# Attention with the values' products in two column tiles, another order of transfers, and part of VectorE's work elsewhere

## The chip, the core and the metric

One core of a Trainium2 chip runs the whole program. The time is device microseconds of one execution; the figure compared is the median of several executions. A profiled execution has a trace besides, with the start, the length and the releaser of nearly every instruction on the five engines: TensorE (PE; its weight loads are PEld), VectorE (DVE), ScalarE (ACT), GpSimd (POOL) and SyncE (SP, which here only issues transfers).

## The reference

Three layers in a row, all in float32 (the last one's weights come as float64): attention with a window of 128 keys and four sink keys, for 2 batches of 768 positions with 8 heads of 64; a layer of experts, in which each of the 1536 tokens goes to one of 8 experts of 192 places each, in the order of the sorted gate logits; and a dense layer with SiLU.

```
scores = q @ k.T / 8, kept where key < 4 or 0 <= pos_q - pos_k < 128
a = softmax(scores);  x = a @ v                      # [2, 8, 768, 64] -> [1536, 512]
logits = x @ w_gate                                  # [1536, 8]
for idx in argsort(-logits.flatten()):               # greedy, capacity 192 per expert
    tok, e = idx // 8, idx % 8
    if not assigned[tok] and counts[e] < 192: assign tok to e
y[tok] = relu(x[tok] @ w1[e]) @ w2[e]
h = y @ w_in;  out = (h / (1 + exp(-h))) @ w_out
```

## The kernel before

Attention works on 12 tiles of 128 positions with 8 heads each; a half-tile is four heads. One loop (in `attention_band`) runs over steps n, one per head, and each step issues the stages of several heads, each some steps behind the scores:

- `s_mm`, every fourth step: the scores of four heads, in 64x64 tiles of TensorE, 32 matmuls (16 for the first tile of a batch, which has no tile before it), into two PSUM banks out of a ring of four (`s`).
- `s_merge` and `s_max`: VectorE merges the two parts of the window (`copy_predicated`) and takes mask and maximum. `s_exp`, two steps later: ScalarE's exponential.
- `tr`, five steps later: TensorE transposes the exponentials; after four heads, `tr_out` copies them to SBUF on ScalarE (`at`), and GpSimd's two selects cut them into the own tile's part (`atd`) and the tile before's (`at`). `sink_tr`, once per tile: the sinks' exponentials are transposed, and a copy to `ats` is made on VectorE.
- `pv`, 13 steps later, one head a step: one or two matmuls of 128 columns of weights with 73 columns of `va` streamed. The 73 are 64 values, 8 logits (value times gate weights, so that the logits come out of the same product) and a one for the softmax's sum. After the fourth head one product with `vsr` adds the four sinks of all four heads.
- `finish`, after each half-tile: VectorE takes the reciprocal `rv` of the sums (L388), the 32 logits times `rv` (`lw`, L384), the sum of the logits over heads (L391), and the 256 values times `rv` (`x`, L395), which goes to memory with a transfer.

Short work of ScalarE and VectorE that is due soon is put into the deques `act_now` and `dve_now`, other work into `act_bg` and `dve_bg`; `feed` issues one piece at a time at fixed places of a step. `vw`, `vw_tr` and `sinks` (due at the steps of `VWS`) make the logit columns of `va` for two tiles at a time. `warm` issues matmuls on zeros in the first steps.

The float64 weights of the dense layer come as raw pieces in hooks of the same loop, and are unpacked there on VectorE in passes of 128x512 words (`s0` removes the sign, then multiplies and bitwise passes, `s1` on). `FIRST`, `EVEN` and `ODD` are the steps of these hooks: `W.load` asks for a raw piece, `W.unpacked` issues a pass. `load` and `load_v` issue the transfers of a tile on SyncE's queue.

Behind attention the routing repeats an iteration `nit` times with the logits `L_sb`; `foresee` is a hint on the branch that ends it. Then tokens are gathered, and the experts' and the dense layer's matmuls fill the rest.

Of the kernel before, what the change touches and what calls it, by code (L numbers as in the profile page):

```python
# [21 lines left out]
P = 128  # L22
# [5 lines left out]
E = 8  # L28
# [164 lines left out]
WARM = (8,) + (2,) * 5  # L193


def attention_band(tc, qd, kd, va_d, vt_d, vs_d, sel_d, wbd_d, eye_d, n_sink, ident, x_d, L_sb, pp, hooks={}):
    nc = tc.nc
    with ExitStack() as ctx:
# [14 lines left out]
        def load_v(i):  # L213
            b, j = divmod(i, NB)
            if i % 2 == 0:
                vts[i // 2] = wp.tile([P, 4, 2, P], F32, name="vt", bufs=2)
            nc.sync.dma_start(vts[i // 2][:, :, i % 2], vt_d[b, j])
            nc.sync.dma_start(va[:, j], va_d[b, j])
# [131 lines left out]
        def pv(n):  # L350
            i, h = divmod(n, H)
            b, j = divmod(i, NB)
            g, r = divmod(h, 4)
            if r == 0:
                if (i, g) == (NT - 1, 0):
                    X[i, g] = misc(HH * VW).rearrange("p (h v) -> p h v", h=HH)
                else:
                    X[i, g] = pp.tile([P, HH, VW], F32, name="X", bufs=PB["X"])
# [7 lines left out]
            nc.tensor.matmul(X[i, g], ats[i % 2], vsr[b][:, g * HH:(g + 1) * HH], start=False, stop=True,  # L366
                             skip_group_check=True)
            finish(i, g)

        def finish(i, g):  # L370
# [17 lines left out]
            dve_now.append(lambda: nc.vector.reciprocal(rv, xp[:, :, D + E]))  # L388
            dve_now.append(weigh)
            if g == 1:  # L390
                dve_now.append(lambda: nc.vector.tensor_reduce(L_sb[:, i], lw.rearrange("p h e -> p e h"), AX.X,  # L391
                                                               OP.add))
            if i < NT - 2:
                def out():
                    nc.vector.tensor_tensor(x[:, hs], xp[:, :, :D], rv.unsqueeze(2).to_broadcast([P, HH, D]), OP.mult)  # L395
                    act_bg.extend(send)
                dve_bg.append(out)
# [40 lines left out]
        act_now, act_bg, act_late, dve_now, dve_bg = (deque() for _ in range(5))  # L438
        warm(WARM[0])
# [88 lines left out]
class Route:  # L528
# [188 lines left out]
    def run(self, L, idx, nit, more, bg=lambda k: None, speculate=lambda: None):  # L717
        self.place(self.psum("s"))
        for k in range(nit):
            bg(k)  # L720
            if k + 1 == nit:
                self.foresee("settled")
            self.iterate(NA, HOLD[0] if k == 0 else 0)
            self.warm(HOLD[1 + (k + 1 == nit)])
            if k == 0:
                self.scaled()
        bg(nit)
        badi = self.result(idx)
        speculate()
        self.warm(HOLD[3])  # L730
        self.further(badi, L, idx, more, speculate, "settled")
# [155 lines left out]
FIRST, EVEN, ODD = 18, (34, 40, 46, 58, 64, 70, 76, 82, 86), (*range(27, 49, 2), *range(53, 93, 2))  # L887


class Weights:  # L890
# [28 lines left out]
    def unpack(self, k, half):  # L919
# [4 lines left out]
        for part in range(2):  # L924
# [599 lines left out]
def fused(tc, a, out, n_sink, window):  # L1524
    nc = tc.nc
    with ExitStack() as ctx:
# [18 lines left out]
        with rest:  # L1545
# [3 lines left out]
            if banded(n_sink, window):  # L1549
                pp = rest.enter_context(tc.tile_pool(name="p", bufs=1, space=PSUM))  # L1550
                hooks = {NT * H // 2: [load_route]}
                for k in range(W.raws):
                    hooks.setdefault(FIRST + 2 * k, []).append(W.load)
# [147 lines left out]
```

## Time and profile before

| | us |
|---|---|
| median of three runs | 552.18 (551.89 to 552.75) |
| the profiled execution's own time | 551.16 |
| its span in the trace | 549.4 |
| PE busy (share of the span) | 529.3 (96%) |
| VectorE busy | 352.0 (64%) |
| ScalarE busy | 293.2 (53%) |
| GpSimd busy | 228.5 (42%) |

The busy times are means over stages that differ: attention ends at about 98 us, the routing iterations and the gathers of tokens at about 131, the experts at about 285, and the dense layer takes the rest. TensorE's 96% says nothing about which engine the others wait for in attention; this is read from busy times by stretch and from the instructions in order of time. In an order of time, the time of one instruction is its own length, and the start of the next may lie inside it; where one engine's instructions follow each other without a wait, the distance of their starts is what one costs.

### The profile page before, as it was taken

How to read it: one execution, taken by the hardware profiler on the slowest of the kernel's cores; microseconds unless marked ns; L12 is line 12 of the kernel's file. 1: busy time of each engine (PE TensorE's matmuls, PEld its weight loads, DVE VectorE, ACT ScalarE, POOL GpSimd, SP SyncE). 2: the span in 40 equal slices, each digit the busy share in tenths (PEclk: the TensorE clock that was granted, in tenths of full speed). 3: DMA queues.
4: the chain of work that ended last, by engine and by line, in shares of the span. 5: the costliest groups of instructions: out<-in, count | busy, mean ns of one | idle time of the engine just before them, and what ended most of it. 6: DMA issues, size and time to landing. Idle time of an engine off the chain costs nothing.

```text
span 549.4 us, 10689 instructions
## 1 busy us (share of the span) xinstructions
PE 529.3 (96%) x3901; PEld 480.2 (87%) x3901; DVE 352.0 (64%) x983; ACT 293.2 (53%) x576; POOL 228.5 (42%) x219
## 2 busy tenths in 40 slices
PE   8999899878999999999999999999999999999995
PEld 4788688757999999999999998988889899888884
DVE  3798999672443443343338898777979776853523
ACT  4555555655776776786654564443544344443330
POOL 4444354377699999999992000000000000000304
PEclk9999999799999999999999999999999999999999
DMA  7999843155466666666760554553676756265502
GB/s 213 359 391 320 278 162 110 39 197 161 153 210 217 226 227 219 227 222 222 226 184 1 209 201 161 215 161 108 219 263 219 277 173 225 91 241 203 202 17 115
DMA packets 43939, 107.98 MB, mean 197 GB/s; under 512 B 4650, under 2 KB 12458, under 8 KB 43884
## 3 DMA queue, kind: packets, MB, share of 16 engines
q1 hardware_dynamic: 41696, 100.88, 54.1%
q0 software_dynamic: 1920, 6.29, 3.3%
q8 instruction: 31, 0.51, 0.4%
q14 instruction: 24, 0.20, 0.1%
q10 hardware_dynamic: 268, 0.10, 0.1%
HBM read 86.81 MB, written 20.45 MB: 195 GB/s over the span
## 4 chain that ended last, share of the span: by engine, by line
PE 69%; issue 4%; POOL 2%; DMA 1%; ACT 0%; DVE 0%; POOLq 0%; another core or an unknown queue 0%; DVEq 0%; ACTq 0%
PE h L1294 21%; PE acc L1416 21%; PE mm L1200 9%; PE m L1223 8%; PE mm L1203 4%; PE m L1226 4%; POOL out L1387 2%; PE mm L1223 1%; PE mm L1159 1%; DMA row<-x_d,idx 1%; PE mm L1226 1%; PE m L1200 0%; POOLq L1697 0%; PE m L1159 0%; ACT wr L976 0%
## 5 line engine op out<-in xcount | busy, mean ns | idle before, releaser
L979 POOL TENSOR_TENSOR wr<-raw,wr 128x1024 fp32r<-128x1024 f32 x64 | 150.8, 2386 | 9.1 <-ACT wr L976 8.9
L1416 PE MATMUL acc<-wr,gt 128*128 128x512 f32 x576 | 145.4, 395 | 0.0
L1416 PEld LDWEIGHTS acc<-wr,gt 128*128 128x128 f32 x576 | 107.3, 188 | 19.5
L1387 POOL DMA_INDIRECT out<-raw,idx x12 | 11.6, 964 | 241.4 <-DVE raw L1428 241.1
L1294 PE MATMUL h<-x,wr 128*128 128x384 f32 x528 | 101.3, 338 | 0.0
L1294 PEld LDWEIGHTS h<-x,wr 128*128 128x128 f32 x528 | 93.8, 188 | 4.0 <-DVE keep L1328 0.2
L1200 PE MATMUL mm<-xg,wr 128*128 128x384 f32 x248 | 72.4, 360 | 0.5 <-DVE xg L1174 0.3
L976 ACT ACTIVATE wr<-raw 128x1024 fp32r<-128x1024 f32 x64 | 66.8, 1052 | 2.4 <-DMA raw<-in_w 1.3
L1223 PE MATMUL m<-ht,wr 128*128 128x384 f32 x224 | 66.0, 361 | 0.0
L1203 PE MATMUL mm<-xg,wr 128*128 128x192 f32 x248 | 62.2, 251 | 0.0
L1226 PE MATMUL m<-ht,wr 128*128 128x192 f32 x224 | 56.2, 251 | 0.0
L1475 DVE TENSOR_TENSOR gt<-keep,gt 128x384 fp32r<-128x384 f32 x64 | 39.1, 612 | 26.7 <-ACT gt L1281 26.6
L301 ACT ACTIVATE A<-t,nm 128x132 f32<-128x132 f32 x96 | 36.4, 401 | 24.7 <-DVE nm L292 24.4
L1181 DVE TENSOR_TENSOR mm<-mm,t 128x384 f32<-128x384 f32 x33 | 18.7, 566 | 45.2 <-ACT t L1180 45.2
L1200 PEld LDWEIGHTS mm<-xg,wr 128*128 128x128 f32 x248 | 46.5, 188 | 1.2 <-DVE xg L1174 0.7
L1203 PEld LDWEIGHTS mm<-xg,wr 128*128 128x128 f32 x248 | 47.3, 191 | 0.0
L1280 ACT ACTIVATE keep<-keep 128x384 f32<-128x384 f32 x30 | 15.8, 526 | 54.0 <-DVE keep L1328 53.9
L1226 PEld LDWEIGHTS m<-ht,wr 128*128 128x128 f32 x224 | 42.8, 191 | 0.0
L1223 PEld LDWEIGHTS m<-ht,wr 128*128 128x128 f32 x224 | 42.0, 188 | 0.0
L323 POOL TENSOR_SCALAR_AFFINE_SELECT atd<-at 128x512 f32<-128x512 f32 x24 | 17.0, 708 | 50.8 <-ACT at L321 45.7
L1294 PE MATMUL h<-xn,wr 128*128 128x384 f32 x180 | 36.8, 339 | 0.0
L1294 PEld LDWEIGHTS h<-xn,wr 128*128 128x128 f32 x180 | 32.6, 188 | 2.6
(198 smaller groups left out, 931.9 us busy)
## 6 DMA issues: line engine op xcount, KB each, us to landing
raw<-in_w SPq DMA_DIRECT2D x64, 512.0 KB, 4.7
sums_d<-os SPq DMA_DIRECT2D x36, 256.0 KB, 2.0
xn<-mix_d SPq DMA_DIRECT2D x12, 768.0 KB, 5.7
raw<-in_wi SPq DMA_DIRECT2D x16, 512.0 KB, 4.8
raw<-in_wo SPq DMA_DIRECT2D x16, 512.0 KB, 4.7
os<-sums_d SPq DMA_DIRECT2D x24, 256.0 KB, 3.1
mix_d<-xn SPq DMA_DIRECT2D x6, 768.0 KB, 4.7
va<-in_va SPq DMA_DIRECT2D x12, 292.0 KB, 6.1
```

Of the source, the lines that this page charges most:

```text
L301: nc.scalar.activation(A[i][:, h], t, AF.Exp, bias=nm, scale=-1.0)
L976: nc.scalar.activation(w[:, 0, sl], src(), AF.Copy)
L979: (nc.vector if k in self.late else nc.gpsimd).tensor_tensor(w[:, 1, sl], src(), w[:, 0, sl].bitcast(F32), OP.subtract)
L1181: nc.vector.tensor_tensor(h, h, t, OP.add)
L1200: nc.tensor.matmul(mm[:, b, :2 * CAP], w[:, 0, fb, d, o:o + P], x[:, d].rearrange("p a t -> p (a t)"), start=d == 0, stop=False, skip_grou ...
L1203: nc.tensor.matmul(mm[:, b, :CAP], w[:, 1, fb, d, o:o + P], x[:, d, 0], start=False, stop=d == 3, skip_group_check=True)
L1223: nc.tensor.matmul(mm[:, d % 2, :2 * CAP], w[:, 0, d // 2, f, o:o + P], ht[:, f].rearrange("p a t -> p (a t)"), start=c == 0 and f == 0, s ...
L1226: nc.tensor.matmul(mm[:, d % 2, :CAP], w[:, 1, d // 2, f, o:o + P], ht[:, f, 0], start=False, stop=last, skip_group_check=True)
L1294: nc.tensor.matmul(h, w(a, d), x(b, d), start=start and d == 0 and k == 0, stop=d == n - 1 and k == 2, skip_group_check=True)
L1387: i = nc.gpsimd.indirect_dma_start(out=out, out_offset=bass.IndirectOffsetOnAxis(ap=idx[:, t // 3, t % 3:t % 3 + 1], axis=0), in_=o, in_of ...
L1416: nc.tensor.matmul(a, gt[:, u, ts], w[:, v, 2 * p + i], start=(p, i, k) == (0, 0, 0), stop=(p, i, k) == (1, 1, 2), skip_group_check=True)
L1475: later.popleft()()
```

## The change

The values' products of four heads are issued together, at every fourth step, ahead of the next scores (`pv`); each product of 128 output rows becomes two of 64, on two column tiles of TensorE. The sinks' product (`pv_sink`) follows behind the scores. The sinks' copy goes to ScalarE for all tiles. For the tiles up to the eighth, `finish` copies the whole half-tile to SBUF on ScalarE (`xc`), VectorE takes the reciprocal of the copy, GpSimd makes both products, and the sum over heads follows four steps later; the last four tiles keep the old way. The sign removal of the early pieces becomes an absolute value on ScalarE. `load_v` is split, its transfers are put into another order, and the raw pieces of the weights are asked for at other steps, the later ones later. The warm-up matmuls are cut into five pieces each, the steps of `vw` and `vw_tr` are shifted by two and one, and the branch hint is given one iteration sooner.

```diff
-    VWS[2 * H * m + 5], VWS[2 * H * m + 8] = [((m,), 0)], [((m,), 1)]
+    VWS[2 * H * m + 7], VWS[2 * H * m + 9] = [((m,), 0)], [((m,), 1)]
...
-        load_v(0)
+        load_vt(0)
+        load_va(0)
         nc.sync.dma_start(vsf[0][:96], vs_d[:96, 0])
-        load_v(1)
+        load_vt(1)
         load(2)
+        load_va(1)
...
-                nc.tensor.matmul(idle, zero[:, :P], zero, start=True, stop=True)
+                for sl in map(slice, WE, WE[1:]):
+                    nc.tensor.matmul(idle[:, sl], zero[:, :P], zero[:, sl], start=True, stop=True)
...
-            if i < NT - 1:
-                dve_now.appendleft(lambda: nc.vector.tensor_copy(ats[i % 2][:96], tp))
-            else:
-                act_now.appendleft(lambda: nc.scalar.activation(ats[i % 2][:96], tp, AF.Copy))
+            act_now.appendleft(lambda: nc.scalar.activation(ats[i % 2][:96], tp, AF.Copy))
...
-            o = X[i, g][:, r]
-            nc.tensor.matmul(o, d[:, r], va[:, j, h], start=r == 0, stop=False, skip_group_check=True)
-            if j:
-                nc.tensor.matmul(o, f[:, r], va[:, j - 1, h], start=False, stop=False, skip_group_check=True)
-            if r < 3:
-                return
+            for r in range(HH):
+                for t, c in ((d, j), (f, j - 1))[:2 if j else 1]:
+                    for q in (slice(HB), slice(HB, P)):
+                        nc.tensor.matmul(X[i, g][q, r], t[:, r, q], va[:, c, h + r], start=r == 0 and t is d,
+                                         stop=False, skip_group_check=True)
+
+        def pv_sink(n):
...
+            if i >= NT - 4:
+...
+            xc = wp.tile([P, HH, VW], F32, name="xc", bufs=3)
+
+            def taken():
+                nc.scalar.activation(xc, xp, AF.Copy)
+                at_step[now[0] + 1].append(over)
+
+            def over():
+                nc.vector.reciprocal(rv, xc[:, :, D + E])
+                for o, w in ((lw, slice(D, D + E)), (x, slice(D))):
+                    nc.gpsimd.tensor_tensor(o[:, hs], xc[:, :, w],
+                                            rv.unsqueeze(2).to_broadcast([P, HH, w.stop - (w.start or 0)]), OP.mult)
+                if g == 1:
+                    at_step[now[0] + 4].append(logits)
                     act_bg.extend(send)
+            act_now.append(taken)
...
+            dve_now.extend(at_step.pop(n, ()))
+            of = n - LP - HH + 1
+            due = of % HH == 0 and 0 <= of < NH
+            if due:
+                pv(of)
-            if n < NH and n % 4 == 0:
+            if n < NH and n % HH == 0:
                 s_mm(n)
+            if due:
+                pv_sink(of)
...
-                if i == 1:
+                if i == 4:
                     nc.sync.dma_start(vsf[1][:96], vs_d[:96, 1])
-                if i + 2 < NT:
-                    load_v(i + 2)
+                if i % 2 == 0:
+                    load_vt(i + 2)
+                    load_vt(i + 3)
                 if i + 3 < NT:
                     load(i + 3)
+                load_va(i + 2)
...
-            if 0 <= n - LP < NH:
-                pv(n - LP)
...
-            if k + 1 == nit:
+            if k + 2 == nit:
                 self.foresee("settled")
...
-FIRST, EVEN, ODD = 18, ...
+FIRST, EVEN, ODD = (17, 25, 33, 45, 53, 60, 67), ...
...
-                nc.vector.tensor_scalar(box[0][:, sl], word(1), 0x7FFFFFFF, None, OP.bitwise_and)
+                if k in self.early:
+                    nc.scalar.activation(box[0][:, sl].bitcast(F32), word(1).bitcast(F32), AF.Abs)
+                else:
+                    nc.vector.tensor_scalar(box[0][:, sl], word(1), 0x7FFFFFFF, None, OP.bitwise_and)
```

TensorE before, in the middle of attention, from the last score of a half-tile on (`tp` are the transposes of the exponentials, `X` the values' products, L366 the sinks' product):

```order
L264 MATMUL s<-kall,qr 64x132
L315 MATMUL tp<-ident,A 128x128
L414 MATMUL s<-ident,vwt 128x128 x2
L361 MATMUL X<-va,atd 128x73
L363 MATMUL X<-va,at 128x73
L366 MATMUL X<-vsr_157,ats_172 128x292
L315 MATMUL tp<-ident,A 128x128
L361 MATMUL X<-va,atd 128x73
L363 MATMUL X<-va,at 128x73
```

One transpose and one head's products take turns until the next scores. TensorE after, at the same place:

```order
L270 MATMUL s<-kall,qr 64x132
L372 MATMUL X<-vsr_156,ats_172 128x292
L321 MATMUL tp<-ident,A 128x128 x2
L442 MATMUL s<-ident,vwt 128x128 x2
L321 MATMUL tp<-ident,A 128x128 x2
L366 MATMUL X<-va,atd 64x73 x2
L366 MATMUL X<-va,at 64x73 x2
```

The last two rows stand four times, once for each head, and then come the next scores: the transposes now stand together, and the products together behind them, in pairs of 64 output rows.

VectorE before, with the reciprocal and the two products of a finished half-tile (`rv`, `lw`, `x`) between score maxima (L292) and merges (L284):

```order
L388 RECIPROCAL rv_902<-X_833 128x4
L292 ISA t_915,nm_916<-s_859,mask_162 128x132
L292 ISA nm_916 128x1
L384 TENSOR_TENSOR lw_901<-X_833,rv_902 128x32
L284 COPY_PREDICATED s_858<-later_158,s_858 128x128
L284 COPY_PREDICATED s_859<-later_158,s_859 128x128
L395 TENSOR_TENSOR x_900<-X_833,rv_902 128x256
L292 ISA t_929,nm_930<-s_858,mask_162 128x132
L292 ISA nm_930 128x1
L933 TENSOR_SCALAR f64_934<-raw_521 128x512
```

VectorE after, at such a place (L977 and L989 are passes that unpack weights):

```order
L989 SCALAR_TENSOR_TENSOR f64_1468<-raw_1021,f64_1468 128x512
L417 RECIPROCAL rv_1587<-xc_1588 128x4
L298 ISA t_1611,nm_1612<-s_1569,mask_162 128x132
L298 ISA nm_1612 128x1
L290 COPY_PREDICATED s_1568<-later_158,s_1568 128x128
L290 COPY_PREDICATED s_1569<-later_158,s_1569 128x128
L298 ISA t_1623,nm_1624<-s_1568,mask_162 128x132
L298 ISA nm_1624 128x1
L977 TENSOR_SCALAR f64_1468<-f64_1468 128x512
```

The reciprocal stays between the maxima and now reads the copy; both products and the sign removal (L933) are gone from this engine. ScalarE after, in a stretch with all three kinds of work that came to it:

```order
L307 ACTIVATE A_1372<-t_1388,nm_1389 128x132
L307 ACTIVATE A_1372<-t_1438,nm_1439 128x132
L352 ACTIVATE ats0_171<-s_1458 96x128
L971 ACTIVATE f64_1468<-raw_1021 128x512
L307 ACTIVATE A_1372<-t_1454,nm_1455 128x132
L307 ACTIVATE A_1372<-t_1465,nm_1466 128x132
L413 ACTIVATE xc_1506<-X_1475 128x292
L327 ACTIVATE at_1516<-tp_1449 128x512
```

Between the exponentials (L307) and the copy of the transposes (L327), which were there, stand the sinks' copy (L352), the sign removal (L971) and the copy of the finished half-tile (L413).

## Rows read from the trace of the kernel before

**Rows 1.** Busy us (instructions) of each engine by stretch; then clock, DMA share, GB/s.

```profile
14.00:30.00 16.00, 14.88 (x231) 13.09 (x231) 12.24 (x71) 9.35 (x29) 6.91 (x15) 1.00 1.07 366
30.00:75.50 45.50, 42.58 (x629) 37.27 (x628) 43.48 (x218) 25.52 (x70) 19.96 (x41) 1.00 0.90 310
75.50:88.00 12.50, 12.21 (x179) 10.45 (x182) 12.48 (x67) 6.88 (x20) 6.01 (x12) 1.00 0.32 111
20.00:40.00 20.00, 19.59 (x295) 17.31 (x296) 17.07 (x94) 11.63 (x32) 8.71 (x19) 1.00 1.05 388
```

**Rows 2.** TensorE in order of time: start, length, line, operation, shape.

```profile
26.69 0.92 PE L264 MATMUL s<-kall,qr 64*64 64x128 f32 x32
27.54 0.33 PE L315 MATMUL tp<-ident,A 128*128 128x128 f32 x1
27.70 0.34 PE L361 MATMUL X<-va,atd 128*128 128x73 f32 x2
...
28.07 0.38 PE L366 MATMUL X<-vsr,ats 97*128 97x292 f32 x1
28.29 0.27 PE L315 MATMUL tp<-ident,A 128*128 128x128 f32 x1
28.40 0.27 PE L344 MATMUL s<-ident,a 128*96 128x128 f32 x1
28.51 0.34 PE L361 MATMUL X<-va,atd 128*128 128x73 f32 x2
...
28.91 0.27 PE L315 MATMUL tp<-ident,A 128*128 128x128 f32 x1
...
30.02 1.45 PE L264 MATMUL s<-kall,qr 64*64 64x128 f32 x32
```

**Rows 3.** TensorE in order of time, in a first tile of a batch.

```profile
48.72 0.68 PE L264 MATMUL s<-kall,qr 64*64 64x132 f32 x16
49.33 0.33 PE L315 MATMUL tp<-ident,A 128*128 128x128 f32 x1
...
50.39 0.64 PE L403 MATMUL s<-vt,wbd 128*32 128x256 f32 x8
```

**Rows 4.** VectorE in order of time: start, length, line, operation, shape.

```profile
41.27 0.18 DVE L384 TENSOR_TENSOR lw<-X,rv 128x32 f32<-128x32 f32 x1
41.37 0.48 DVE L284 COPY_PREDICATED s<-later,s 128x128 f32<-128x128 int32 x2
41.76 0.41 DVE L395 TENSOR_TENSOR x<-X,rv 128x256 f32<-128x256 f32 x1
42.10 0.28 DVE L292 CUSTOM_DVE_ANT_0 t<-s,mask 128x132 f32<-128x132 f32 x1
...
42.31 0.42 DVE L933 TENSOR_SCALAR f<-raw 128x512 int32<-128x512 int32 x1
42.64 0.28 DVE L292 CUSTOM_DVE_ANT_0 t<-s,mask 128x132 f32<-128x132 f32 x1
...
45.38 0.28 DVE L346 CAST ats<-s 96x128 fp32r<-96x128 f32 x1
45.58 0.28 DVE L292 CUSTOM_DVE_ANT_0 t<-s,mask 128x132 f32<-128x132 f32 x1
```

**Rows 5.** Groups by line, 30 to 88 us: count, busy us, mean ns, idle before.

```profile
L326 POOL TENSOR_SCALAR_AFFINE_SELECT at<-at 128x512 f32<-128x512 f32 x14 | 10.6, 759 | 1.0
L321 ACT ACTIVATE at<-tp 128x512 f32<-128x512 f32 x15 | 8.9, 593 | 8.9 <-PE tp L315 8.9
```

**Rows 6.** TensorE in order of time, with idle time before and its releaser.

```profile
16.60 0.90 PE L264 MATMUL s<-kall,qr 64*64 64x128 f32 x28 [0.52 <-DVE ats L346]
```

**Rows 7.** TensorE behind the routing, in order of time.

```profile
129.85 0.66 PE L1159 MATMUL mm<-ident,row 128*128 128x128 f32 x4 [0.54 <-DMA row<-x_d,idx]
```

**Rows 8.** A select on GpSimd and a pass on VectorE beside it.

```profile
36.02 0.63 POOL L323 TENSOR_SCALAR_AFFINE_SELECT atd<-at 128x512 f32<-128x512 f32 x1 [0.92 <-ACT at L321]
36.16 0.77 DVE L937 TENSOR_SCALAR f<-f 128x512 f32<-128x512 f32 x1
```

More of the change, by code (lines that the diff above doesn't have):

```diff
@@ L1 @@
 import math
-from collections import deque
+from collections import defaultdict, deque
 from functools import partial
@@ L190 @@
 for m in range(1, NT // 2):
-    VWS[2 * H * m + 5], VWS[2 * H * m + 8] = [((m,), 0)], [((m,), 1)]
+    VWS[2 * H * m + 7], VWS[2 * H * m + 9] = [((m,), 0)], [((m,), 1)]
 PB = {"s": 4, "tp": 2, "X": 2}
-WARM = (8,) + (2,) * 5
+WARM, WE = (8,) + (2,) * 5, (0, 104, 208, 312, 412, 512)
 def attention_band(tc, qd, kd, va_d, vt_d, vs_d, sel_d, wbd_d, eye_d, n_sink, ident, x_d, L_sb, pp, hooks={}):
@@ L211, in load, with load_vt, load_va @@
                 nc.sync.dma_start(Q[i][:, p:p + step], qd[b, j][:, p:p + step])
-        def load_v(i):
-            b, j = divmod(i, NB)
+        def load_vt(i):
+            if i >= NT:
+                return
             if i % 2 == 0:
                 vts[i // 2] = wp.tile([P, 4, 2, P], F32, name="vt", bufs=2)
-            nc.sync.dma_start(vts[i // 2][:, :, i % 2], vt_d[b, j])
-            nc.sync.dma_start(va[:, j], va_d[b, j])
+            nc.sync.dma_start(vts[i // 2][:, :, i % 2], vt_d[i // NB, i % NB])
+        def load_va(i):
+            if i < NT:
+                nc.sync.dma_start(va[:, i % NB], va_d[i // NB, i % NB])
         load(0, 1)
@@ L352, in pv @@
             b, j = divmod(i, NB)
[L353 to L358, printed above, removed]
-            f, d = AT[i, g]
-            o = X[i, g][:, r]
-            nc.tensor.matmul(o, d[:, r], va[:, j, h], start=r == 0, stop=False, skip_group_check=True)
-            if j:
-                nc.tensor.matmul(o, f[:, r], va[:, j - 1, h], start=False, stop=False, skip_group_check=True)
-            if r < 3:
-                return
-            nc.tensor.matmul(X[i, g], ats[i % 2], vsr[b][:, g * HH:(g + 1) * HH], start=False, stop=True,
+            g = h // HH
+            if (i, g) == (NT - 1, 0):
+                X[i, g] = misc(HH * VW).rearrange("p (h v) -> p h v", h=HH)
+            else:
+                X[i, g] = pp.tile([P, HH, VW], F32, name="X", bufs=PB["X"])
+            f, d = AT[i, g]
+            for r in range(HH):
[4 more added lines that the diff above has]
+        def pv_sink(n):
+            i, h = divmod(n, H)
+            g = h // HH
+            nc.tensor.matmul(X[i, g], ats[i % 2], vsr[i // NB][:, g * HH:(g + 1) * HH], start=False, stop=True,
                              skip_group_check=True)
@@ L386, in weigh, with logits, out @@
                     act_late.extend([partial(scaled, r) for r in range(HH)] + send)
[L388 to L395, printed above, removed]
+            def logits():
+                nc.vector.tensor_reduce(L_sb[:, i], lw.rearrange("p h e -> p e h"), AX.X, OP.add)
+            if i >= NT - 4:
+                dve_now.append(lambda: nc.vector.reciprocal(rv, xp[:, :, D + E]))
+                dve_now.append(weigh)
+                if g == 1:
+                    dve_now.append(logits)
+                if i < NT - 2:
+                    def out():
+                        nc.vector.tensor_tensor(x[:, hs], xp[:, :, :D], rv.unsqueeze(2).to_broadcast([P, HH, D]),
+                                                OP.mult)
+                        act_bg.extend(send)
+                    dve_bg.append(out)
+                return
+            xc = wp.tile([P, HH, VW], F32, name="xc", bufs=3)
[7 more added lines that the diff above has]
+                                            rv.unsqueeze(2).to_broadcast([P, HH, w.stop - (w.start or 0)]), OP.mult)
+                if g == 1:
+                    at_step[now[0] + 4].append(logits)
                     act_bg.extend(send)
-                dve_bg.append(out)
+            act_now.append(taken)
         def vw(m, os=(0, 1)):
@@ L438, in attention_band @@
         act_now, act_bg, act_late, dve_now, dve_bg = (deque() for _ in range(5))
+        at_step, now = defaultdict(list), [0]
         warm(WARM[0])
@@ L442, in attention_band @@
             i, h = divmod(n, H)
-            if n < NH and n % 4 == 0:
+            now[0] = n
+            dve_now.extend(at_step.pop(n, ()))
[4 more added lines that the diff above has]
+            if n < NH and n % HH == 0:
                 s_mm(n)
+            if due:
+                pv_sink(of)
             if n < len(WARM) - 1:
@@ L886 @@
 PLAIN, MIXED = "uuddduuddd", "ududududududu"
-FIRST, EVEN, ODD = 18, (34, 40, 46, 58, 64, 70, 76, 82, 86), (*range(27, 49, 2), *range(53, 93, 2))
+FIRST, EVEN, ODD = (17, 25, 33, 45, 53, 60, 67), (34, 40, 46, 58, 64, 70, 76, 82, 86), (*range(27, 49, 2), *range(53, 93, 2))
 class Weights:
@@ L1551, in fused @@
                 hooks = {NT * H // 2: [load_route]}
-                for k in range(W.raws):
-                    hooks.setdefault(FIRST + 2 * k, []).append(W.load)
+                for n in FIRST:
+                    hooks.setdefault(n, []).append(W.load)
                 for n in sorted({*EVEN, *ODD}):
```

1 line of the change is left out of this document (added).

## The prediction, made before the changed kernel was run

> **What bounds the kernel now.** I read the clock and busy shares by stretch first, then the two fullest engines' instructions in order of time, then what the other engines' operations cost. Everything behind 98 us (the routing iterations, the gathers, the expert and dense layers) is left as it was by the change, apart from one branch hint, so the question is how much sooner attention hands over. In its middle, 30.0 to 75.5 us, VectorE is busy 43.5 of 45.5 us and TensorE 42.6, at the full clock [rows 1]; those 45.5 us hold twelve half-tiles of four heads, 3.79 us each. From 14 to 30 us VectorE has slack (12.2 of 16.0) and TensorE little (14.9); from 75.5 to 88 us VectorE has none (12.48 of 12.50). So in the middle two engines bind almost equally: freeing one alone gives next to nothing, and the change frees both.
>
> On TensorE one half-tile without waits takes 3.33 us, 26.69 to 30.02 [rows 2]: the scores 0.85, the sink product 0.22 (28.07 to 28.29), a transpose 0.11 (28.29 to 28.40), and the values' products of one head 0.40 (28.51 to 28.91; four records of 73 columns, each with a 128-column load). Two score groups of the twelve are stretched, the first to 1.45 us against 0.92 [rows 2]: there TensorE waits for VectorE to free a score bank. Without these 1.0 us TensorE needs 42.6 - 1.0 = 41.5 us for the twelve.
>
> **The values' products (TensorE).** Before, four heads cost 4 x 0.40 = 1.60 us. After, each product is two of 64 output columns, on two column tiles: twice the records (32 of 73 columns), which gains only if the two tiles run at the same time. The trace has no such pair of 128-row tiles, but near ones. Scores of a first tile: 16 records of 132 columns in 0.61 us (48.72 to 49.33), so each of four tiles streams 4 x 132 = 528 columns [rows 3]; scores of another tile: 32 records in 0.85 us, 784 columns per tile [rows 2]. The difference, 0.24 us for 256 columns, is 0.94 ns a column, and 0.115 us stay fixed. And the eight records of 256 columns on four column tiles (128 rows each) take 0.64 us [rows 3], where one after the other they would need eight times 256 x 0.94 ns, 1.9 us: column tiles over the same rows do stream together. Two tiles with 16 records each: 1168 columns x 0.94 + 0.115 = 1.21 us. I take this; it saves 0.39 us per half-tile. The ends: if a record of half the load costs half of today's 0.10, 16 x 0.05 + 0.115 = 0.92 us; if the tiles load one at a time, 32 x 0.05 + 0.115 = 1.72 to 1.9 us, which is a loss. Half-tiles of a first tile (no second source) gain some 0.05. Sum over the twelve: 10 x 0.39 + 2 x 0.05 = 4.0, so TensorE's need falls to 37.5 us.
>
> The fixed 0.115 us stands for the change between tile shapes, and rows show it again: the transpose behind the scores takes 0.16 until the next product where others take 0.11 [rows 2]. [...] There is now one more change per half-tile, which the 0.115 holds.
>
> **VectorE.** Its operations are issued back to back, so what counts is the time to the next start [rows 4]: the logit product 0.10 (41.27 to 41.37), the normalising product 0.34 (41.76 to 42.10), the sink copy 0.20 (45.38 to 45.58), sign removal 0.33 (42.31 to 42.64). Eight of twelve tiles lose the two products (0.44 a half-tile), all but the last tile lose the sink copy, and the eight pieces of sign removal go. In the middle: 12 x 0.44 + 6 x 0.20 + 6 x 0.33 = 8.5 us, so VectorE needs 43.5 - 8.5 = 35.0. The reciprocal stays, now reading a copy.
>
> **Where that work goes.** ScalarE gets a copy of 128x292 per half-tile, the sink copies and eight 128x512 sign removals. Its 128x512 copy takes 0.59 [rows 5]: 0.3 to 0.6 for the 292, up to 0.6 for the signs, so 12 x 0.45 + 6 x 0.25 + 6 x 0.55 = 10 us on top of 25.5 busy, 36 of the 40 us then left. GpSimd gets two products; its 128x512 select takes 0.76 [rows 5], so 0.4 to 0.8 for the 256 wide and 0.2 to 0.3 for the 32 wide, some 11 us on 20.0. Neither is the fullest, but no engine has much room any more. Cover for the longer way to the logits: they are reduced four steps later, a half-tile of time; the last four tiles keep the old way, so nothing is added at the end.
>
> **What twelve half-tiles take.** Today 2.0 us more than the fuller engine's 43.5. With 37.5 and 35.0, and two more hand-overs in the ring, I allow 2.5: 40.0, a gain of 5.5 us (no loss at all would be 8.0; a loss of 4 would be 4.0). **Before them** (14 to 30 us): two half-tiles with two sources, 0.8, and two waits in one score group, 0.8 together, the larger one 0.52 for the sink copy [rows 6], which now comes from ScalarE; of 1.6 I take 1.3, since other chains are just behind (at least 0.5). **Behind them**, 75.5 to 88 us, VectorE alone binds: two sink copies and one sign removal, 0.7 us. From 88 us on: nothing; there the counts of the first iteration now stand behind a whole group of products and its sink instead of behind three heads, and the group is shorter by as much.
>
> **Edits at no price.** The warm-up matmuls are cut in five but stream the same 512 columns. The transfers: tile data are asked for three tiles ahead, and weights' raw pieces later; from 14 to 75.5 us the queues move 366 and 310 GB/s [rows 1], 20.0 MB; at 388, the mean of the 20 us from 20.0 on [rows 1], that would take 51.5 us where the forecast leaves 54.7, so transfers don't bind, though not by much. The hint one iteration sooner: behind the branch TensorE's transposes wait for the gathered rows, not for code (0.54 us, released by the transfer [rows 7]), and that covers it; without this cover it could give some tenths.
>
> Sum: 5.5 + 1.3 + 0.7 = 7.5 us against the profiled execution's own 551.16 us (span 549.4), so 543.7; the median of the runs lies 1.0 above the profiled one, so **544.7 us**.
>
> **Rivals.** (a) *The hand-overs eat the gain.* VectorE's reciprocal now waits for ScalarE's copy, which waits for the sink product, which stands behind the group's products and the next scores on TensorE; score maxima are queued behind that reciprocal, and exponentials behind the copy. And GpSimd's work slows VectorE's weight unpacking: a 128x512 pass takes 0.77 us when a select runs beside it (36.02 and 36.16 us) [rows 8], another one 0.42 (42.31 us) [rows 4]. With 0.3 us of this per half-tile VectorE needs 38.6, and with a loss of 3.5 the twelve take 42: gain 3.4 + 1.0 + 0.2, 547.6 us. For it: four engines all at 85% or more. Against: the reciprocal stands half a microsecond of other VectorE work behind the scores. [...] (b) *The tiles load one at a time: slower.* Place: the two 64-column loads of each pair, over the same 128 rows. Price: 1.9 us per four heads instead of 1.60. TensorE then needs 41.5 + 10 x 0.3 + 2 x 0.28 = 45.1, with its 2.0 of loss 47.1 for the twelve, 1.6 more than now; before them 0.3 is gained, behind them 0.7 less 0.9 in the last products: 553.7 us. It decides from about 1.75 us per four heads on. Against it: the column-tiled rows of 256 columns [rows 3]; for it, that these hide short loads behind long streams, and 73 columns don't. [...] (c) *Half overlap*: 1.5 us per four heads, TensorE hardly better, only the waits and the end gain: 551 us.
>
> **How the numbers follow.** Forecast 0.66, (a) 0.16, (b) 0.10, (c) 0.08. A run of three rounds tells about 0.2% (1.1 us) from no change. Faster by more: the forecast, (a) and half of (c): 0.86. Within: the rest of (c) and a little of (b), 0.05. Slower: 0.09. The forecast's own bounds: gains of 4.0 + 0.5 + 0.5 (547.2) to 8.0 + 1.6 + 0.7 (541.9), a little lower if records cost 0.05. The range takes in (a) and stops short of (b): 540.5 to 550.5.
>
> **What would show it.** Right: four heads of products in 1.1 to 1.3 us; half-tiles of 3.2 to 3.4 us in the middle; VectorE with idle gaps ended by TensorE or ScalarE; the first routing iteration some 7 us sooner, and everything behind it shifted by the same. Wrong: products of four heads at 1.6 us or more; reciprocals that wait half a microsecond each; or a routing stage that starts sooner but ends no sooner, because weights come late.

## The result: slower by 0.7% where 1.4% faster was forecast

The changed kernel takes 556.07 us (median of nine executions, 553.24 to 557.16) against 551.89 us of before in the same rounds; the ratio is 1.007, with a 95% interval of 1.0049 to 1.0091. The forecast was 544.7 us, within 540.5 to 550.5, with 0.09 for slower. The profiled execution took 556.25 us, its span is 554.5 us.

Busy time by stretch after, as in [rows 1] (columns as there), and two stretches of 6 us behind them:

```profile
14.00:30.00 16.00, 13.52 (x289) 10.55 (x278) 10.39 (x60) 9.80 (x32) 7.95 (x19) 0.99 1.06 368
30.00:75.50 45.50, 41.62 (x830) 33.88 (x831) 37.22 (x182) 32.08 (x96) 31.19 (x65) 0.93 0.92 317
75.50:88.00 12.50, 11.08 (x227) 8.47 (x223) 11.59 (x57) 7.99 (x24) 6.83 (x13) 1.00 0.40 138
...
28.00:34.00 6.00, 4.19 (x68) 3.62 (x69) 2.26 (x12) 3.37 (x10) 2.12 (x4) 0.72 0.59 231
56.00:62.00 6.00, 5.91 (x93) 5.13 (x93) 3.88 (x15) 2.12 (x8) 2.12 (x5) 0.72 1.00 355
```

The work went where the change sent it: VectorE's 43.48 us of the middle are 37.22 now, ScalarE has 32.08 instead of 25.52, GpSimd 31.19 instead of 19.96. But the twelve half-tiles take 43.2 us (32.66 to 75.83) instead of 45.4 (30.02 to 75.46), where 40.0 were forecast, and the granted clock, 1.00 before in all three stretches, is 0.72 on average in two stretches of 6 us.

The values' products on TensorE after (start, length, line, operation, shape), to be held against 0.40 us a head in [rows 2]:

```profile
24.95 0.35 PE L366 MATMUL X<-va,atd 128*64 128x73 f32 x4
25.12 0.30 PE L366 MATMUL X<-va,at 128*64 128x73 f32 x4
...
25.89 0.30 PE L366 MATMUL X<-va,at 128*64 128x73 f32 x4
26.11 0.38 PE L270 MATMUL s<-kall,qr 64*64 64x128 f32 x4
```

32 records stand between 24.95 and 26.11: four heads cost 1.16 us, and 1.21 were forecast. So the column tiles do what was expected of them, and the loss must lie elsewhere. Two milestones show where. The last scores of attention end at 89.29 us (before 88.78), and the last product of the routing at 126.56 (125.55): attention and routing lose 1.0 us where they should gain 7.5. From there to the first transposes of gathered rows it takes 7.92 us (before 4.30): 3.6 us more, in a stretch in which nothing seemed to be changed. TensorE at these places, after:

```profile
88.37 0.92 PE L270 MATMUL s<-kall,qr 64*64 64x128 f32 x32
...
126.37 0.19 PE L882 MATMUL X<-neg,N 128*128 128x8 bf16 x2
...
130.51 4.18 PE L1195 MATMUL mm<-wr 128*128 128x512 f32 x9 [3.05 <-DVEq L780]
134.48 1.06 PE L1199 MATMUL mm<-ident,row 128*128 128x128 f32 x4
```

And before (its first transposes, at 129.85, are in [rows 7]):

```profile
87.87 0.91 PE L264 MATMUL s<-kall,qr 64*64 64x128 f32 x32
...
125.36 0.19 PE L845 MATMUL X<-neg,N 128*128 128x8 bf16 x2
...
126.98 2.33 PE L1155 MATMUL mm<-wr 128*128 128x512 f32 x9 [0.53 <-DVEq L743]
```

L780 (L743 before) is the branch that ends the routing. TensorE waits 3.05 us instead of 0.53, for VectorE's sequencer; its granted clock falls from 1.00 to 0.50 in that wait (0.50 from 129 to 135 us), and the same nine warm-up matmuls, which stand ahead of the transposes, then take 4.18 us instead of 2.33. VectorE's own rows at this line (count, duration in ns, first and last start in us), after, and before:

```profile
L780 DVEq EVENT_SEMAPHORE  x2: 21/21/21, 130.3 to 130.5; - x2
...
L780 DVEq COMPARE_BRANCH  x1: 72/72/72, 127.2 to 127.2; - x1
```

```profile
L743 DVEq EVENT_SEMAPHORE  x2: 21/21/21, 126.8 to 126.9; - x2
...
L743 DVEq COMPARE_BRANCH  x1: 72/72/72, 126.2 to 126.2; - x1
```

VectorE branches at 127.2 and does its next step at 130.3; before, 0.6 us lay between the two.

### The profile page after: what moved, and what is told of

It reads as the page before. It is cut to its first block, busy times and chain, and to the rows that moved or that the text cites. A ratio compares the mean times of both kernels' runs of the same rounds, so it can differ in the third digit from the quotient of the medians.

```text
span 554.5 us, 11517 instructions
## 1 busy us (share of the span) xinstructions
PE 526.0 (95%) x4325; PEld 474.8 (86%) x4325; DVE 342.4 (62%) x932; ACT 301.9 (54%) x611; POOL 242.7 (44%) x251
## 4 chain that ended last, share of the span: by engine, by line
PE 68%; issue 4%; POOL 2%; DMA 1%; DVE 0%; ACT 0%; POOLq 0%; another core or an unknown queue 0%; DVEq 0%; ACTq 0%
PE h L1334 21%; PE acc L1456 20%; PE mm L1240 9%; PE m L1263 8%; PE mm L1243 4%; PE m L1266 4%; POOL out L1427 2%; PE mm L1263 1%; PE mm L1199 1%; PE mm L1266 1%; DMA raw<-in_w 1%; POOL wr L1019 0%; POOL row L1157 0%; PE m L1240 0%; POOLq L1737 0%
## 5 line engine op out<-in xcount | busy, mean ns | idle before, releaser
L307 ACT ACTIVATE A<-t,nm 128x132 f32<-128x132 f32 x96 | 35.3, 401 | 11.3 <-DVE nm L298 10.8
L1321 ACT ACTIVATE gt<-keep 128x384 fp32r<-128x384 f32 x64 | 33.7, 527 | 2.0
```

Of the source, the lines that this page charges most:

```text
L307: nc.scalar.activation(A[i][:, h], t, AF.Exp, bias=nm, scale=-1.0)
L1321: nc.scalar.activation(gt[:, 0], h, AF.Copy)
```

## Experiments on the wait behind the branch

**The hint.** It had been moved, so it was undone alone and done alone:

```diff
-            if k + 2 == nit:
+            if k + 1 == nit:
                 self.foresee("settled")
```

> The changed kernel with the branch hint given where it stood before, in the last iteration. Theory A (the hint given sooner costs the gap of 3 us behind the branch in the trace of after): 552 to 553 us, and the matmuls behind the branch start about 1.5 us after the last product of the routing, as in the kernel before. Rival B (the gap comes from the longer instruction stream of TensorE, 848 rows more in attention): no change, 556 us.

> The kernel before with only the hint one iteration sooner. Theory A: 3 to 4 us slower than before, some 555.3 us, all of it behind the branch. Rival B: no change, 552 us.

Measured: 556.26 us (ratio 1.0082, 1.0053 to 1.0112) and 551.51 us (1.0001, 0.998 to 1.0022). Theory A fell: the wait is there with either place of the hint, and the hint alone changes nothing, as the prediction had priced it.

**The place of the branch in TensorE's program.** The page counts transfers of instructions: 31 on queue q8, 0.51 MB, before and 35, 0.57 MB, after, so some 16 KB each, and four more for the 848 additional records of TensorE in the trace (8650 against 7802, so about 250 records to one of them; a row here is one instruction of an engine's program). Two kernels shift TensorE's rows, by the warm-up pieces alone:

```diff
-WE = (0, 104, 208, 312, 412, 512)
+WE = (0, 172, 344, 512)                # e5; e6: five pieces put into the kernel before
```

> The changed kernel with each warm-up matmul cut in three pieces instead of five: 72 rows fewer ahead on TensorE, so that the branch behind the routing lies as many rows past a multiple of 256 (67) as in the kernel before (66; in the changed kernel 139). Theory C (TensorE's instructions come in transfers of 16 KB, 256 rows, and whether the code behind the branch is there in time hangs on where the branch lies among them): the matmuls behind the branch start 0.5 us after it waits for nothing else, not 3 us, they run at the full clock, and the time falls by 3 to 4 us, to 552.5 us. Rival D (the longer stream as such, or the transfers of that time, make the code late): the gap of 3 us stays, 556 us.

> The kernel before with only the warm-up matmuls cut in five pieces, 144 rows more ahead on TensorE, the same columns. Theory C: the branch now lies 210 rows past a multiple of 256, in another place among the transfers of code, and a gap of 3 us behind the branch is likely: 555 us. Rival D (attention's other edits are needed for the gap): 552 us, gap 0.5 us.

e5: 554.44 us (1.0052, 1.0025 to 1.008), and VectorE's wait is unchanged; theory C was wrong for the changed kernel. TensorE's own branch even takes 1.48 us in e5, against 0.41 after, though it now stands where theory C wanted it. e6: 555.16 us (1.0077, 1.0044 to 1.0111), though the routing ends as before (125.66 us). In e6 it is TensorE's own branch that takes 2.9 us, 0.48 in the kernel before:

```profile
L744 DVEq EVENT_SEMAPHORE  x2: 21/21/21, 126.9 to 127.0; - x2
...
L744 PEldq COMPARE_BRANCH  x1: 2881/2881/2881, 125.8 to 125.8; - x1
```

So each engine can be late behind the branch, by itself (VectorE by 3.1 us after, TensorE's branch with 2.9 us in e6), and on TensorE 144 rows more with the same work were enough.

**VectorE's rows.** The change takes 79 rows off VectorE's program ahead of the branch, which stands at row 529 instead of 608. They were put back as writes of one element, or VectorE got the hint too:

```diff
+        for _ in range(79):
+            nc.vector.memset(spare, 0.0)
```

```diff
-        pe = [mybir.EngineType.PE]
+        pe = [mybir.EngineType.PE, mybir.EngineType.DVE]
```

> The changed kernel with 79 one-element writes on VectorE in its idle first 5 us, so that its branch behind the routing lies at the same row as in the kernel before (608 instead of 529, target 827). Theory J (the wait of 3 us behind the branch is VectorE's: it branches at 127.31 us, its next instruction comes at 130.34, and TensorE waits for it and then runs its warm-up matmuls at half clock; whether VectorE's code is there depends on the row of the branch): VectorE goes on 0.5 us after its branch, TensorE starts with it, and the time falls by 3.5 to 4.5 us, to some 552 us, no better than before. Rival K (VectorE waits for something else behind the branch): gap and time stay, 556 us.

> The changed kernel with the branch hint given to VectorE as well as to TensorE. Theory J (VectorE's code comes late): the hint brings it in time, VectorE goes on within 0.6 us of its branch, 552 us. Rival K: no change, 556 us; so too if the hint has no effect on VectorE's code.

f1 (553.66 us; 1.0017, 0.9993 to 1.0041), VectorE in order of time, and its rows at the branch:

```profile
1.14 8.92 DVE L343 MEMSET spare_v<- 1x1 f32 x79
10.12 0.29 DVE L298 CUSTOM_DVE_ANT_0 t<-s,mask 128x132 f32<-128x132 f32 x1
```

```profile
L783 DVEq EVENT_SEMAPHORE  x2: 21/21/21, 129.9 to 130.0; - x2
...
L783 DVEq COMPARE_BRANCH  x1: 72/72/72, 129.3 to 129.3; - x1
```

The wait is gone (0.6 us), as theory J says; but 79 writes at 113 ns overran the idle time, and the first maximum came at 10.12 instead of 6.10 us, so f1 gives back part of it at the start. f2 changed nothing (555.71 us; 1.0064, 1.004 to 1.0089; VectorE goes on 3.6 us after its branch): a hint given to VectorE has no effect here.

The trace counts the instruction transfers of each queue. Those that begin in VectorE's wait in the changed kernel, from 127.2 to 130.4 us (packets, MB, share of the transfer engines' time; q8 is the queue that grew with TensorE's rows):

```profile
q8 instruction: 1, 0.02, 2.2%
q14 instruction: 2, 0.02, 1.9%
```

So code does come in during the wait, but no transfer of it begins in the wait's last 1.5 us (from 128.9 us on). Whether VectorE waits for any of these transfers isn't shown.

## Experiments on attention

**Single waits.** After, ScalarE and TensorE at 28 us (idle time and its releaser in brackets), and TensorE at two later waits:

```profile
28.81 0.66 ACT L971 ACTIVATE f<-raw 128x512 f32<-128x512 f32 x1 [2.70 <-DMA raw<-in_wi]
```

```profile
29.81 0.77 PE L321 MATMUL tp<-ident,A 128*128 128x128 f32 x2 [2.00 <-ACT A L307]
...
50.89 0.32 PE L351 MATMUL s<-ident,a 128*96 128x128 f32 x1 [0.68 <-POOL a L313]
...
56.09 0.38 PE L452 MATMUL s<-va,sel 4*96 4x64 f32 x2 [1.21 <-ACT va L445]
```

ScalarE's first sign removal waits for the raw piece, the exponentials are queued behind it, and TensorE runs dry for 2.0 us; its mean granted clock from 28 to 34 us is 0.72. From 56 to 62 us it is the same behind waits of 0.68 and 1.21 us. Three kernels (all but e8 with the hint as before) each took one cause away:

```diff
-                if k in self.early:                                       # e3: signs on VectorE
-                    nc.scalar.activation(..., AF.Abs)
+                nc.vector.tensor_scalar(..., OP.bitwise_and)
...
-    VWS[2 * H * m + 7], VWS[2 * H * m + 9] = ...                          # e4
+    VWS[2 * H * m + 5], VWS[2 * H * m + 8] = ...
...
-FIRST = (17, 25, 33, 45, 53, 60, 67)                                      # e8, with load_vt, load_va
+FIRST = (18, 20, 22, 24, 26, 28, 30)                                      # and vsf[1] as before
```

> Hint as before, and the sign removal of the early weights back on VectorE; all else as in the changed kernel. Theory A (ScalarE stands 2.7 us behind the first raw piece, exponentials are queued behind it, TensorE runs dry for 2.0 us and its granted clock then falls to half): ScalarE's wait is gone, no fall of the clock near 30 us, about 4 us faster than the same kernel with the signs on ScalarE, some 548.5 us. Rival B (VectorE then waits for the same piece with maxima queued behind it, and TensorE runs dry all the same): 552 to 553 us and the clock falls near 30 us as before.

> Hint as before, and the products for the logit columns (two tiles at a time) back at their earlier steps, 5 and 8 instead of 7 and 9. Theory A (the sinks' product of the second batch, due at step 58, waits 1.2 us for columns that now come one step ahead of it; TensorE's clock falls after that wait): no such wait near 55 us, no fall of the clock near 57 us, 2 to 3 us faster than the same kernel with the later steps, some 550 us. Rival B (the wait of 0.7 us for GpSimd's part of the sinks at 50 us is enough, or VectorE is what TensorE waits for there): within 0.5 us of it, 552.5 us.

> The changed kernel with the transfers in the order of before: values and their columns tile by tile, the second batch's sinks early, raw pieces asked for from step 18 on every second step. Theory G (the new order makes the first raw piece and a values' transfer land late, TensorE waits for them and its clock falls): ScalarE's wait of 2.7 us for the raw piece is under 1.2 us, no fall of the clock before 50 us, routing ends 3 us sooner, 553 us. Rival H (the engines' new hand-overs make the waits, not the order of transfers): the clock falls as in after, 556 us.

555.30 us (1.0058, 1.003 to 1.0085), 554.77 (1.006, 1.0036 to 1.0085) and 555.25 (1.0072, 1.0027 to 1.0118): none can be told from the changed kernel, nor e3 and e4 from e1. The wait for the first raw piece is gone from e3's profile, but TensorE waits at 12 us for a transfer and the clock falls there instead:

```profile
12.51 0.60 PE L431 MATMUL s<-vt,wbd 128*32 128x128 f32 x8 [2.03 <-DMA vt<-in_vt]
```

```profile
12.00:20.00 8.00, 7.39 (x97) 5.01 (x101) 3.56 (x17) 3.51 (x12) 1.04 (x4) 0.57 1.08 358
28.00:34.00 6.00, 6.00 (x149) 5.33 (x147) 5.31 (x28) 4.36 (x15) 4.68 (x11) 1.00 0.72 234
```

That wait isn't the edit's. e1, which has the signs on ScalarE, shows it too, and later a wait of 1.65 us for exponentials queued behind another raw piece:

```profile
12.47 0.43 PE L431 MATMUL s<-vt,wbd 128*32 128x128 f32 x8 [1.78 <-DMA vt<-in_vt]
...
45.21 0.63 PE L321 MATMUL tp<-ident,A 128*128 128x128 f32 x2 [1.65 <-ACT A L307]
```

After and e1 differ by the hint alone, which comes much later in the program. So which of these waits appears differs from execution to execution, and a wait that is missing from one profile isn't thereby shown to be cured.

In e8's profile the clock is 1.00 from 8 to 98 us, and its last scores still ended at 88.41 us: with the falls gone, the gain had not come back, so they were not the main loss there.

**The column tiles.** Taken out of the changed kernel, and put alone into the kernel before:

```diff
-                    for q in (slice(HB), slice(HB, P)):
-                        nc.tensor.matmul(X[i, g][q, r], t[:, r, q], va[:, c, h + r], ...)
+                    nc.tensor.matmul(X[i, g][:, r], t[:, r], va[:, c, h + r], ...)
```

> The changed kernel with the values' products as one matmul of 128 output rows again, in the new order. Theory E (two column tiles keep TensorE less busy, so its clock falls at short waits that did no harm before): four heads cost 1.6 us instead of 1.16, the mean clock is back at 0.99 and the time is at or below 553 us. Rival F (the waits alone make the clock fall, whatever the shape of the products): the mean clock stays at 0.98, 555 to 557 us.

> The kernel before with only the values' products of four heads together in two column tiles and the sinks' product behind the scores; VectorE's branch lies at row 588 (76). Theory N (in the middle VectorE binds almost as much as TensorE, so TensorE's 0.4 us per half-tile brings little alone): the last scores of attention end within 1.5 us of before (88.8 us), 550.5 to 552 us. Rival (column tiles make the gain alone): 4 us sooner, 548 us. Rival (they cost the clock): mean clock 0.98, 553 us or more.

e7: 560.90 us (1.0158, 1.0106 to 1.0211); theory E fell, since the clock was no better (0.974 of the span) and the last scores ended at 94.81 us, 5.5 us later than after. Four heads cost 1.84 us there (30.11 to 31.95), more than the 1.60 of before that was expected:

```profile
30.11 0.34 PE L365 MATMUL X<-va,atd 128*128 128x73 f32 x2
...
31.95 0.91 PE L270 MATMUL s<-kall,qr 64*64 64x128 f32 x32
```

So part of the 5.5 us is the new order with whole products, not the lack of column tiles alone.

g3: the last scores end at 89.01 us, 0.2 us later than before, as theory N says; but its 554.74 us (1.0066, 1.0034 to 1.0097) and its clock of 0.981 are the numbers of the second rival. In its profile the time is lost behind the scores: 1.4 us up to the end of the routing and 2.2 from there to the first transposes, where TensorE's own branch takes 2.4 us:

```profile
L749 PEldq COMPARE_BRANCH  x1: 2361/2361/2361, 127.3 to 127.3; - x1
```

From 24 to 98 us the mean clock is 0.98 in g3 (1.00 before), but also in e2 and e6, which have no column tiles, so the tiles aren't shown to cost the clock. Alone they bring attention nothing; beside less work on VectorE they bring something (e7), how much isn't shown.

**The normalising.** Put back on VectorE for all tiles, then with 24 rows of padding, then with transfers or waits mended on top:

```diff
-            if i >= NT - 4:
+            if i >= 0:
                 dve_now.append(lambda: nc.vector.reciprocal(rv, xp[:, :, D + E]))
```

> The changed kernel with the normalising of all tiles as before: reciprocal, logits and values' product on VectorE straight from PSUM, no copy on ScalarE, no products on GpSimd. Theory L (the way over ScalarE and GpSimd costs as much in waits as it frees on VectorE): the waits for GpSimd's part of the sinks near 51 and 67 us go, and the last score group of attention ends at 88 to 89 us as in after (89.3) or sooner. Rival M (freeing VectorE is what the change gains): the last score group ends 3 us later, near 92 us. In both the wait behind the branch stays.

> Normalising on VectorE as before, and 24 one-element writes on VectorE in its first idle time (113 ns each, 2.7 us of 4.9), so that its branch lies at row 584. Branches at rows 96 past a multiple of 128 went on at once, at 17, 48 and 99 they waited 3 to 3.6 us; if the good places reach from about 62 to 97, row 584 (72) is one. Theory L (normalising over two engines cost some 3 us) with theory J (late code): VectorE goes on 0.5 us after its branch and the time is 548 to 549 us, the first one below before. Rival: the wait stays, 552 us.

f3: 552.28 us (1.0009, 0.9985 to 1.0034), the last scores at 86.14 us: 3.2 sooner than after, though VectorE has more to do. Two of the groups by line between 30 and 88 us on VectorE show one thing that came with the change (count, busy us, mean ns), after, and f3:

```profile
L985 DVE SCALAR_TENSOR_TENSOR f<-raw,f 128x512 int32<-128x512 int32 x8 | 7.0, 869 | 0.0
...
L977 DVE TENSOR_SCALAR f<-f 128x512 f32<-128x512 f32 x7 | 4.2, 605 | 0.0
```

```profile
L985 DVE SCALAR_TENSOR_TENSOR f<-raw,f 128x512 int32<-128x512 int32 x8 | 5.5, 686 | 0.0
...
L977 DVE TENSOR_SCALAR f<-f 128x512 f32<-128x512 f32 x8 | 3.3, 418 | 0.0
```

The same passes take 183 and 187 ns longer in the kernel in which GpSimd makes the products. Single rows show it: a pass of VectorE beside a product of GpSimd (after), and the same pass with GpSimd idle (e1, where GpSimd is busy for 0.09 of the 2 us from 44 to 46):

```profile
44.30 0.84 DVE L977 TENSOR_SCALAR f<-f 128x512 f32<-128x512 f32 x1
...
44.25 0.62 POOL L419 TENSOR_TENSOR x<-xc,rv 128x256 f32<-128x256 f32 x1
```

```profile
44.90 0.43 DVE L977 TENSOR_SCALAR f<-f 128x512 f32<-128x512 f32 x1 [1.35 <-ACT f L971]
```

So part of what left VectorE came back as slower unpacking. That this is what made the kernel slower isn't shown: in the twelve half-tiles VectorE has slack after (35.90 us busy of 43.17, row below).

g1: 547.97 us (0.9934, 0.9911 to 0.9956), faster than both kernels, with the branch at VectorE's row 584. TensorE behind the branch in f3, then in g1, and g1's middle:

```profile
128.34 4.18 PE L1195 MATMUL mm<-wr 128*128 128x512 f32 x9 [3.60 <-DVEq L780]
```

```profile
122.19 2.33 PE L1198 MATMUL mm<-wr 128*128 128x512 f32 x9 [0.53 <-DVEq L783]
```

```profile
30.00:75.50 45.50, 41.47 (x880) 33.15 (x874) 42.38 (x222) 30.68 (x87) 22.20 (x44) 1.00 0.91 322
```

f3 to g1 is 4.3 us by the medians. In the two profiles, 3.7 us of the difference stand between the routing's last product and the first transposes (8.48 and 4.77 us): the price of VectorE's late step with the low clock behind it. Another 3.1 us stand ahead of it, where f3's profiled execution waits 1.52 us at 12.44 us, with the clock at half behind that, and g1's doesn't; this is one of the waits that come and go. After to f3 is 3.8 us by the medians: the price of normalising over two more engines, as a whole; ScalarE's copies, GpSimd's products and the waits that came with them weren't separated. The rest of the change is worth 3.9 us against before.

> As g1, with the transfers in the order of before as well. If the new order makes waits (values' transfers late at 11 us, raw piece late at 26 us) that let the clock fall: 1 to 2 us below g1, 547 us. Rival (the new order is what keeps later transfers in time): 1 us or more above g1, 549.5 us or more.

> As g1, with the logit columns at their earlier steps, the second batch's sinks two steps later and the first unpacking two hooks later. If the waits for the raw piece (up to 2.7 us) and for the columns (1.0 us) are still on the path: 1.5 to 2.5 us below g1, 546.5 us. Rival (others stand just behind them): within 0.7 us of g1.

g2: 549.58 us (0.9966, 0.9946 to 0.9987), 1.6 us above g1, but the two intervals overlap: the new order of transfers is rather a gain, which isn't shown. g4: 548.33 us (0.9916, 0.9879 to 0.9953), as g1. No wait for a raw piece is left in its profile, and mending it brought nothing that can be told from noise. An earlier kernel meant to beat both kept the normalising of the change and set 79 rows of padding, with its branch three rows further on:

> A version meant to beat both: the changed kernel with VectorE's 79 rows of padding, the logit columns at their earlier steps with the second batch's sinks two steps later, and the first unpacking two hooks later, behind the landing of the first raw piece. If the waits named so far are what the change lost (3 us behind the branch with the low clock after it, 2.0 us for the raw piece, 1.2 us for the columns, and the low clock after each): 546 to 549 us. If the low clock comes back at other waits: 551 to 553 us.

554.77 us (1.0048, 1.0025 to 1.007): VectorE's wait of 3.5 us was back, at row 611 instead of 608. Over the eighteen kernels, VectorE went on after 0.6 us at rows 72, 74, 76 and 96 past a multiple of 128 (eight kernels), and after 2.9 to 3.7 us at 17, 19, 23, 25, 48 and 99 (ten). When the branch comes doesn't sort them: the late ones branch at 124.5 to 133.9 us, the prompt ones at 121.4 to 129.3. That the multiple of 128 is what counts isn't shown; it only describes these rows.

## Why the prediction was wrong, step by step

Two steps failed, one ahead of the branch that ends the routing and one behind it. By the profiles the kernel missed the forecast by some 12.5 us (556.25 and 543.7); 8.5 of them stand ahead of the end of the routing (7.5 of gain forecast, 1.0 lost) and 3.6 behind the branch.

- **"Everything behind 98 us is left as it was"** failed. The instructions there are the same, but VectorE's shorter program puts its branch at another row: 3.6 us from before to after, 3.7 between f3 and g1. The cover that was weighed, TensorE waiting for gathered rows rather than for code [rows 7], was TensorE's alone, and it was weighed for the hint, not for the number of rows ahead of the branch. The late steps behind the branch took 1.5 to 3.7 us on TensorE (e5, g3, e6, e7) and 2.9 to 3.7 on VectorE. That the row of the branch decides is shown by shifting rows alone (e6 on TensorE, 0.48 to 2.88 us; f1 on VectorE, 3.1 to 0.6). That what comes late is code is only inferred from it and from the transfers in the wait; no run shows it.
- **The engines' shares were right, ScalarE's somewhat high.** The twelve half-tiles, from the scores at step 32 to those at step 80, after:

```profile
32.66:75.83 43.17, 39.29 (x804) 31.95 (x802) 35.90 (x175) 30.23 (x89) 29.85 (x62) 0.95 0.94 323
```

TensorE's 39.29 us are at a mean clock of 0.95, by estimate 0.05 x 43.2 = 2.2 us lost, so 37.1 against the forecast 37.5 (where 42.6 - 1.0 is 41.6, not 41.5, a slip without weight). VectorE has 35.9 for 35.0, ScalarE 30.2 for 36, GpSimd 29.9 for 31. Four heads of products cost 1.16 us against 1.21. Rival (b) is refuted: 32 records, each with a load over the same rows as its neighbour's, take 1.16 us, not 1.9.

- **The allowance for hand-overs, 2.5 us, was mis-sized.** The twelve half-tiles take 43.2 us, 45.4 before; 40.0 were forecast. TensorE is idle for 3.9 of them (43.17 - 39.29) instead of 2.5, and the low clock takes 2.2 us by that estimate, for which the sum had no term. With the normalising back on VectorE they still take 42.0 us (f3) and 41.9 (g1), at a clock of 1.00 and with 4.2 and 3.8 us of TensorE idle, so 40.0 wasn't reached in any of these profiles.
- **Before the twelve, 1.3 us of gain became a loss of 2.6.** At 26.11 us the scores are still 0.6 ahead of before (26.69 [rows 2]); then the wait for the raw piece, with the low clock behind it, makes one half-tile 6.55 us long (26.11 to 32.66). Behind the twelve nothing came of the 0.7.
- **Rival (a), with 0.16, came true in size; its mechanism only in part.** f3 prices the normalising at 3.8 us where rival (a) had 2.9. Its slower unpacking is there, with 183 and 187 ns a pass (after against f3). But its reciprocals that wait for the copy are not. The reciprocals after, and the idle time of VectorE just before them (what ended it, us in total, times):

```profile
L417 DVE RECIPROCAL rv<-xc x16: 164/172/179, 18.6 to 75.2; 128x4 f32<-128x4 f32 x16
...
  ACT xc L413: 0.5, 1
```

One of sixteen waited. TensorE's waits were others: for exponentials behind a raw piece, for GpSimd's part of the sinks, for the logit columns. How these and the low clock make up the 3.8 us stays open.

- **"Transfers don't bind"** held for the rate, not for the single transfer: the raw piece came 1.1 us later than before (its first reader starts at 28.81 us instead of 27.75), and on ScalarE, ahead of exponentials, that cost 2.0 us of TensorE. Before, VectorE had waited 1.0 us for the same piece with TensorE still supplied. In e1 it was a later piece, with 1.65 us. What it cost in the whole stays open, since e3, e4 and e8 are within the noise of after.
- **The low clock was not in the prediction at all.** All nine executions of after have a mean clock of 0.976 to 0.982, and the profiled one of before 0.993. After, it falls behind waits of TensorE of 2.00 us (0.50 from 30 to 32 us), 1.21 (0.50 from 58 to 60) and 3.05 (0.50 from 129 to 135), though not behind each one: TensorE waits 1.15 us up to 11.63 us, and the clock stays at 1.00 from 10 to 18. It makes a wait cost more than its length: behind the branch 1.85 us more for nine matmuls (4.18 against 2.33).
- **The hint** was as priced. The warm-up's pieces do have a price, as rows (e6, 1.0077). The median was put 1.0 us above the profiled execution; it lies 0.2 below (556.07 and 556.25).

## What to carry to other kernels

Where a program branches at run time, count how many rows an edit adds or removes on each engine ahead of the branch, and look at each engine's first step behind it: there a few us can appear that no edit put there (3.1 us on VectorE after, 0.6 before), and some cheap rows can remove them (24 of them from f3 to g1: TensorE's wait for VectorE's sequencer goes from 3.60 to 0.53 us). Which row is a good one was found here by trying, and a later edit can undo it (f4). Moving work off a full engine can cost more than it brings: here the way over ScalarE and GpSimd cost 3.8 us (f3). Measure the rest of the change without it. And compare two profiles of nearly the same program before a single wait is called the cause.

## What the runs showed of the hardware

- VectorE went on 0.6 us or 2.9 to 3.7 us after the same taken branch, by the row at which it stood; 79 rows alone decided it (529 after, 608 in f1), and in f4, which has other edits too, three rows more (611) had the wait again. TensorE's branch took 0.4 to 0.5 us or 1.5 to 3.7 (1.48 in e5, 2.36 in g3, 2.88 in e6, 3.66 in e7).
- A branch hint one iteration sooner changed nothing (e2, 551.51 us against 552.02), and a hint for VectorE had no effect on its wait (f2, 3.6 us).
- On two column tiles over the same 128 rows the products of four heads took 1.16 us (after, 24.95 to 26.11 us), where the 128-wide form in the same order took 1.84 (e7, 30.11 to 31.95).
- A 128x512 pass of VectorE that took 0.43 us with GpSimd idle (e1, at 44.90 us) took 0.84 beside a 128x256 product of GpSimd (after, at 44.30).
- A write of one element cost VectorE 113 ns (79 in 8.92 us, f1), as much as the 128x32 product of the logits (0.10, [rows 4]).
